# A Trainium2 attention-and-MLP kernel: another engine issues the folded-weight transfers, and some weight loads lose their fixed place in the order

## The chip, the cores and the metric

The kernel runs on one core of one Trainium2 chip. A core has five engines with instruction streams of their own: TensorE (PE in the rows; PEld is its weight load), VectorE (DVE), ScalarE (ACT), GpSimd (POOL) and SyncE (SP). Each runs its instructions in order and waits for the others on semaphores. Transfers run on 16 DMA engines; an instruction stream only issues them, and a wait that a transfer has before it can start is waited out by the engine that issues it. The metric is the device time of one execution in microseconds (us), lower is better.

## The reference

Per batch and head, 32 packed queries attend to 576 keys and values; the 576 queries then attend to the 32 results. The output, 4608 tokens of 512 features, goes through a gated MLP with RMS normalisation and then through a second MLP:

```python
p_packed = sm_attn(p, k, v)              # 8 batches, 8 heads, 32 x 576, head_dim 64
x = sm_attn(q, p_packed, p_packed)       # 576 x 32; then heads side by side: 4608 x 512
rms = np.sqrt(np.mean(x * x, axis=-1, keepdims=True) + 1e-06)
xn = x / rms * rms_g
g = xn @ w_gate                          # 512 x 1536
x = (g * (1.0 / (1.0 + np.exp(-g)))) * (xn @ w_val) @ w_out
h = x @ w_in                             # 512 x 2048
out = np.maximum(0.01 * h, h) @ w_out2   # 2048 x 512
```

## The kernel before

Every float32 product is made of three matmuls of a high and a low part (`mm3`: high by high, low by high, high by low). So each operand is split: ScalarE copies the high part (`act_copy`, line 129), VectorE or GpSimd subtracts it (line 137). Nearly all matmuls go through line 112 in `mm3`.

**Folded weights.** Attention ends in a product of the softmax weights of 576 queries with 32 packed values for each head. The kernel does not form that output: it multiplies the packed values (`lpw`) into the MLP's gate and value weights first (`pw_piece`) and gives the result, `pw`, to the matmuls `g` and `v` (`gv`), whose moving operand is the transposed softmax weights `ath`. The features come in 6 groups (fg) of 256 for each pair of batches, so n = 0 to 23 counts pair and group. For each n there are four pieces (i = 4n + kt). `pw_piece(i)` does three matmuls into the PSUM bank `pwps`, a ScalarE copy of the high part into the weight tile `w` that it just used, a VectorE subtract of the low part into the same tile, and two transfers, one for each half of the partitions (64 partitions x 4 KB, 256 KB), from `w` into `pw[n, 0]` and `pw[n, 1]`. Line 858 issues these: 96 pieces, 192 transfers. All four pieces of n must have landed before the first `g` matmul of n can run. Tile `w` has four buffers, so that a load of a later `w` (line 764) waits for the landing of the transfers out of an earlier one; `pw` has two buffers per batch of the pair, so the first writers of n + 2 wait for the last `v` of n.

**Stages.** The program has four stages. A (0 to about 530 us): the gated MLP for batches 0 to 3 (n = 0 to 11), in which the attention of these batches and the splitting of all weights of the first MLP and of half of the second (`split_w`, `split_wo`, `split_w2`, with loads on lines 742, 775, 764, 796, 813 and stores on line 655) are interleaved by slots. Z (530 to about 970 us): the second MLP for the first four chunks of 512 tokens, in two halves of its 2048 hidden features (`stage3z`: tiles `zh`, `zr`, `zgf`, `zgh`, `zgl`; `stage4z`: `zo`, `zob`, with partial sums stored to and loaded from `op_dram`), interleaved with the attention of batches 4 to 7 (tiles `s`, `e`, `ta`, `pp`, `xp`, `atf`). C (990 to about 1315 us): the gated MLP for batches 4 to 7 (n = 12 to 23), some 28 us for each n, in four steps of `g`, `v` and `y` (tiles `sg`, `hh`, `hl`, `y_acc`). D (1315 to 1776 us): the second MLP for the other five chunks (`h`, `o`).

**Second MLP's weights.** They are read back split from DRAM in parts of 1 MB (128 x 2048 float32): `load_part`, line 986, two parts for each of `w1[f]` and `w2[f]`, f = 0 to 3. The parts are put on a list, `trickle`, and `drop(1)` takes one at a time: in stage A and C at line 1233 (the fused loop over `g`, `v`, `y`), in Z behind each `stage3z` (the middle part), and in D behind each `stage4` (the last part). In the middle part w1[2], w2[2], w1[3] and w2[3] take the place of w1[0], w2[0], w1[1] and w2[1] in the same buffers. In the rows, w12 is w1[2], w22 is w2[2], and so on; a first digit or two of `zh`, `zo` and the like are the chunk-and-half s = 0 to 7 and then the feature tile m, so that zh410 is s = 4, m = 10.

**What sets the order.** The Python code gives a program order, and the Tile scheduler, which works with a model of the durations, orders each engine's instructions anew. An instruction given to `tc.keep_in_program_order` is pinned: it keeps its place in the program. `load_part` pins every load. SP issues all loads and stores, ScalarE only the 192 transfers of line 858.

Of the kernel before, what the change touches and what calls it, by code (L numbers as in the profile page):

```python
# [8 lines left out]
F32 = mybir.dt.float32  # L9
# [30 lines left out]
def pack_attention_moe_kernel(  # L40
# [14 lines left out]
    nc = tc.nc  # L55
# [50 lines left out]
    def mm3(ps, terms, start=True, stop=True):  # L106
        seq = [t for hi, lo in (("h", "h"), ("l", "h"), ("h", "l")) for t in [(hi, lo)]]
        n = len(terms) * 3
        i = 0
        for a, b in seq:  # L110
            for (lh, ll), (rh, rl) in terms:
                mm = nc.tensor.matmul(  # L112
                    ps,
                    lhsT=lh if a == "h" else ll,
                    rhs=rh if b == "h" else rl,
                    start=start and i == 0,
                    stop=stop and i == n - 1,
                )
                i += 1
        return mm  # L120
# [7 lines left out]
    def act_copy(o, i, scale=1.0):  # L128
        nc.scalar.activation(out=o, in_=i, func=AF.Copy, scale=scale)  # L129
# [6 lines left out]
    def sub(eng, o, a, hi):  # L136
        eng.tensor_tensor(out=o, in0=a, in1=hi.bitcast(F32), op=ALU.subtract)  # L137
# [67 lines left out]
    def bank(name):  # L205
        return psA.tile([P, 1, 512], F32, tag="y", bufs=ybufs, name=name)
# [445 lines left out]
    def flush_store():  # L652
        if stores:
            o, t = stores.pop()
            nc.sync.dma_start(out=o, in_=t.bitcast(F32))
# [67 lines left out]
    def until(done):  # L723
        while not done():
            assert drip
            drain(1)
# [103 lines left out]
    pw = {}  # L830

    def pw_piece(i):
        if i >= NPAIR * NFG * KT:
            return
        until(lambda: ("s", i) in wq)
        n, kt = i // KT, i % KT
        pr = n // NFG
        u, x = kt // 2, kt % 2
        if kt == 0:
            for bb in range(2):  # L840
                pw[n, bb] = mlpa.tile(
                    [P, 2, 2, 2 * G * P], F32R, tag=f"pw{bb}", bufs=2, name=f"pw{n}{bb}"
                )
        w = wq.pop(("s", i))
        wh, wl = w[:, 0, :], w[:, 1, :]
        lh, ll = lpw[pr]
        ps = bank(f"pwps{i}")[:, 0, :]
        mm3(ps, [((lh[:, kt, :], ll[:, kt, :]), (wh, wl))])

        if stores and stores[0][1] is w:  # L850
            flush_store()
        st = w
        act_copy(st[:, 0, :], ps)
        sub(nc.vector, st[:, 1, :], ps, st[:, 0, :])
        for half in range(2):
            bb = half if x == 0 else 1 - half
            hs = slice(64 * half, 64 * half + 64)
            nc.scalar.dma_start(out=pw[n, bb][hs, u].bitcast(F32), in_=st[hs].bitcast(F32))

    hid = {}  # L860

# [2 lines left out]
    def gv(n, bb, c, which, g, ps):  # L864
        w = pw[n, bb]
        ah, al = ath[2 * (n // NFG) + bb]
        cs = slice(c * CH, c * CH + CH)
        if g == 0:
            ps = psA.tile([P, G, 512], F32, tag=which, bufs=1, name=f"{which}{n}{bb}{c}")
        o = (0 if which == "g" else G * P) + g * P  # L870
        fs = slice(o, o + P)
        mm3(
            ps[:, g, :CH],
            [((w[:, u, 0, fs], w[:, u, 1, fs]), (ah[:, u, cs], al[:, u, cs])) for u in range(2)],
        )
        return ps
# [55 lines left out]
    for f_ in weights[:HOLD]:  # L932
# [6 lines left out]
        (split_wo, 0),  # L939
        (split_wo, 1),  # L940
        (pw_piece, 0),
        (pw_piece, 1),
        (split_w, 4),
        (pw_piece, 2),
        (split_w, 5),
        (pw_piece, 3),
# [30 lines left out]

    trickle = []

    def drop(count=1):  # L980
        for _ in range(min(count, len(trickle))):
            trickle.pop(0)()

    def load_part(t, src, k_):
        ks = slice(2 * k_, 2 * k_ + 2)
        ins = nc.sync.dma_start(out=t[:, ks].bitcast(F32), in_=src[:, ks])
        tc.keep_in_program_order(ins)

    def load_w1sb(pool, f, tag=None):
        tags = dict(tag=tag, bufs=1) if tag else {}  # L990
        t = w1[f] = pool.tile([P, 4, 2, 512], F32R, name=f"w1{f}", **tags)
        trickle.extend(lambda k_=k_: load_part(t, w1_dram[f], k_) for k_ in range(2))

    def load_w2sb(pool, f, tag=None):
        tags = dict(tag=tag, bufs=1) if tag else {}
        t = w2[f] = pool.tile([P, 4, 2, 512], F32R, name=f"w2{f}", **tags)
        trickle.extend(lambda k_=k_: load_part(t, w2_dram[f], k_) for k_ in range(2))
# [112 lines left out]
    for si, (n, bb, c) in enumerate(steps):  # L1110
# [20 lines left out]
        if si == 2 * 4 * NFG:  # L1131
# [25 lines left out]
            for z, (s_, m) in enumerate(za):  # L1157
# [7 lines left out]
                if z == 31:  # L1165
                    load_w1sb(zw2, 3, "w1")
                drop(1)
                if z == len(za) - 1:
                    zw2.release()
# [61 lines left out]
        if si == 3 * 4 * NFG + 16:  # L1231
            split_y(NZ)
        if si >= 2 * 4 * NFG or si % 2:
            drop(1)
        gps = gv(n, bb, c, "g", 0, None)
        more_y()
        gv(n, bb, c, "g", 1, gps)
# [93 lines left out]
    for n, (i, m) in enumerate(order):  # L1331
        stage3(i, m)
        if n >= 2:
            stage4(*order[n - 2])
        drop(1)
        if m == 2:
            load_y(i + 1)
        if m == 8:
            split_y(i + 1)
# [41 lines left out]
```

## Time and profile before

| | us |
|---|---|
| median of 3 runs | 1775.86 |
| lowest and highest | 1774.94, 1776.55 |
| profiled execution | 1777.73 |
| its span (first to last instruction) | 1775.9 |
| TensorE busy in it | 1676.8 (94%) |
| TensorE busy in stage A, 530 us | 462.97 |
| in stage Z, 460 us | 449.69 |
| in stage C, 325 us | 315.74 |
| in stage D, 461 us | 448.37 |

TensorE's busy time includes time at a lower granted clock, and what is not busy in it is idle time in front of a matmul. The profiled execution took 1777.73 us, of which 1.83 us lie outside the span, and it is 1.87 us above the median. Stages are windows of the trace at the times given above, which the profile does not name itself. Of a matmul that is issued late, the rows give the idle time of TensorE before it and the producer that ended it.

### The profile page before, as it was taken

To read this page: it belongs to the slowest core of one execution; us is meant where nothing else is said; L and a number is where in the kernel's file an instruction comes from. 1 tells how busy PE (TensorE), PEld (TensorE's weight loads), DVE (VectorE), ACT (ScalarE), POOL (GpSimd) and SP (SyncE) were. 2 spreads that over 40 slices of the span, in tenths; PEclk is the share of its full clock that TensorE was granted. 3 is DMA by queue.
4 is the path that set the end of the run, shared out by engine and by line. 5 is a ranking of instruction groups with operands and counts; after the bars stand their busy time and mean duration, and the time that the engine had idled before them with its cause. 6 is when DMAs were issued, how large, how long until landed. Compare 5 with 4: busy or idle time off the path is not lost.

```text
span 1775.9 us, 24117 instructions
## 1 busy us (share of the span) xinstructions
PE 1676.8 (94%) x9252; PEld 1475.1 (83%) x9252; DVE 911.2 (51%) x1560; ACT 648.7 (37%) x1144; POOL 373.0 (21%) x270
## 2 busy tenths in 40 slices
PE   6778899999899999989998999999999999999997
PEld 5568788989898888878887999989998888888885
DVE  7766788557548877666642244334443323232221
ACT  4344555443325555444332422242222222222221
POOL 2244354533322232212121211311110000000000
PEclk9799999999999999989999999999999999999998
DMA  9675777699948563453237656786635101010000
GB/s 293 204 224 147 226 215 226 204 336 300 362 122 280 166 202 126 150 211 105 69 108 239 193 165 202 218 262 181 175 136 238 32 17 34 15 33 15 12 12 24
DMA packets 95527, 287.85 MB, mean 162 GB/s; under 512 B 13876, under 2 KB 20276, under 8 KB 91316
## 3 DMA queue, kind: packets, MB, share of 16 engines
q1 hardware_dynamic: 80052, 235.96, 39.9%
q10 hardware_dynamic: 15360, 50.34, 11.4%
q8 instruction: 73, 1.20, 0.3%
q14 instruction: 42, 0.34, 0.1%
HBM read 174.85 MB, written 61.08 MB: 133 GB/s over the span
## 4 chain that ended last, share of the span: by engine, by line
PE 69%; DMA 18%; DVE 7%; issue 2%; ACT 2%; ACTq 1%; SPq 1%; POOL 0%; DVEq 0%; POOLq 0%
PE h L112 12%; PE o L112 12%; PE y L112 9%; PE zh L112 8%; PE zo L112 8%; PE g L112 6%; DMA pw<-w 6%; PE v L112 5%; PE pwps L112 2%; PE pp L335 2%; DMA out_dram<-zob 1%; PE s L112 1%; DMA w<-in_moe_w_val_dram 1%; DMA w<-in_moe_w_in_dram 1%; DMA y_dram<-y_acc 1%
## 5 line engine op out<-in xcount | busy, mean ns | idle before, releaser
L112 PE MATMUL y<-hh,wo 128*128 128x288 f32 x1536 | 271.2, 298 | 20.0 <-ACT y_acc L129 8.8
L112 PEld LDWEIGHTS y<-hh,wo 128*128 128x128 f32 x1536 | 226.6, 189 | 27.8 <-ACT y_acc L129 10.1
L137 POOL TENSOR_TENSOR hl<-sg,hh 128x576 fp32r<-128x576 f32 x96 | 140.2, 1460 | 406.6 <-ACT hh L129 397.2
L903 DVE TENSOR_TENSOR y_acc<-y_acc,y 128x288 f32<-128x288 f32 x320 | 141.6, 450 | 151.9 <-PE y L112 151.1
L112 PE MATMUL o<-w,gh 128*128 128x512 f32 x640 | 212.4, 392 | 0.0
L1293 DVE TENSOR_TENSOR gf<-r,h 128x512 f32<-128x512 f32 x80 | 55.0, 687 | 248.7 <-ACT r L129 248.7
L112 PE MATMUL zo<-w,zgh 128*128 128x512 f32 x512 | 172.3, 396 | 1.7 <-ACT zgh L129 1.7
L112 PE MATMUL g<-ath,pw 128*128 128x288 f32 x768 | 144.5, 304 | 25.7 <-DMA pw<-w 19.2
L112 PE MATMUL zh<-zyh,w 128*128 128x512 f32 x512 | 162.2, 394 | 3.1 <-DVE zgf L1049 1.9
L112 PE MATMUL h<-yh,w 128*128 128x512 f32 x640 | 162.5, 393 | 0.5 <-DVE y_acc L903 0.5
L112 PE MATMUL y<-hl,wo 128*128 128x288 f32 x768 | 161.7, 296 | 0.0
L112 PEld LDWEIGHTS g<-ath,pw 128*128 128x128 f32 x768 | 119.0, 193 | 35.4 <-issue 17.1
L112 PEld LDWEIGHTS h<-yh,w 128*128 128x128 f32 x640 | 120.0, 188 | 28.1 <-DVE y_acc L903 0.8
L129 ACT ACTIVATE r<-h 128x512 f32<-128x512 f32 x80 | 47.8, 598 | 261.1 <-PE h L112 261.1
L112 PEld LDWEIGHTS o<-w,gh 128*128 128x128 f32 x640 | 120.1, 188 | 27.2
L112 PE MATMUL v<-ath,pw 128*128 128x288 f32 x768 | 140.8, 300 | 0.6 <-ACT sq L538 0.3
L880 DVE TENSOR_TENSOR sg<-sg,v 128x576 f32<-128x576 f32 x96 | 72.1, 751 | 106.0 <-PE v L112 87.0
L112 PE MATMUL o<-w,gl 128*128 128x512 f32 x320 | 125.0, 391 | 0.0
L112 PEld LDWEIGHTS y<-hl,wo 128*128 128x128 f32 x768 | 123.0, 189 | 0.1
L129 ACT ACTIVATE hh<-sg 128x576 fp32r<-128x576 f32 x96 | 65.6, 683 | 150.5 <-DVE sg L880 133.7
L112 PEld LDWEIGHTS v<-ath,pw 128*128 128x128 f32 x768 | 116.5, 191 | 2.0 <-DVE sg L880 0.8
L1239 ACT ACTIVATE sg<-g 128x576 f32<-128x576 f32 x96 | 62.5, 651 | 148.8 <-PE g L112 110.4
(158 smaller groups left out, 3002.6 us busy)
## 6 DMA issues: line engine op xcount, KB each, us to landing
pw<-w ACTq DMA_DIRECT2D x192, 256.0 KB
w<-w_dram SPq DMA_DIRECT2D x72, 512.0 KB
w<-w_dram SPq DMA_DIRECT2D x32, 1024.0 KB
wo<-wo_dram SPq DMA_DIRECT2D x36, 512.0 KB
w_dram<-w2s SPq DMA_DIRECT2D x32, 512.0 KB
w_dram<-w SPq DMA_DIRECT2D x24, 512.0 KB
y_dram<-y_acc SPq DMA_DIRECT2D x32, 288.0 KB
w<-in_moe_w_in_dram SPq DMA_DIRECT2D x16, 512.0 KB
```

The costliest lines, as they stand in the source:

```text
L112: mm = nc.tensor.matmul(ps, lhsT=lh if a == "h" else ll, rhs=rh if b == "h" else rl, start=start and i == 0, stop=stop and i == n - 1,)
L129: nc.scalar.activation(out=o, in_=i, func=AF.Copy, scale=scale)
L137: eng.tensor_tensor(out=o, in0=a, in1=hi.bitcast(F32), op=ALU.subtract)
L335: nc.tensor.matmul(pp[:, 0, :256], lhsT=st["a1T"][:, j // 3, j % 3, :], rhs=vr[:, :, j, :], start=j == 0, stop=j == NJ - 1,)
L880: nc.vector.tensor_tensor(out=hf, in0=sg, in1=vps[:, :, :CH], op=ALU.mult)
L903: pace[:] = [nc.vector.tensor_tensor(out=ya, in0=ya, in1=pv, op=ALU.add).ins]
L1239: nc.scalar.activation(out=sg, in_=gps[:, :, :CH], func=AF.Silu)
L1293: pace[:] = [nc.vector.tensor_tensor(out=gf, in0=r, in1=ps, op=ALU.max).ins]
```

## The change

There are two edits. In `pw_piece` the two transfers of a piece are issued by SP (`nc.sync`) and no longer by ScalarE. And `load_part` no longer pins its load; `drop` pins it if it is told to, which only the fused loop does. So the loads that are dropped in the middle part (Z) and in the last part (D) are free for the scheduler to place, and those of the fused loop stay pinned.

```diff
-            nc.scalar.dma_start(out=pw[n, bb][hs, u].bitcast(F32), in_=st[hs].bitcast(F32))
+            nc.sync.dma_start(out=pw[n, bb][hs, u].bitcast(F32), in_=st[hs].bitcast(F32))
...
-    def drop(count=1):
+    def drop(count=1, pin=False):
         for _ in range(min(count, len(trickle))):
-            trickle.pop(0)()
+            ins = trickle.pop(0)()
+            if pin:
+                tc.keep_in_program_order(ins)
...
-        ins = nc.sync.dma_start(out=t[:, ks].bitcast(F32), in_=src[:, ks])
-        tc.keep_in_program_order(ins)
+        return nc.sync.dma_start(out=t[:, ks].bitcast(F32), in_=src[:, ks])
...
         if si >= 2 * 4 * NFG or si % 2:
-            drop(1)
+            drop(1, pin=True)
```

ScalarE's stream falls from 1296 to 1106 rows of the order, SP's rises from 515 to 711. The scheduler answers with another order on the other engines too: on TensorE some 2000 lines of the difference, small displacements of `g`, `v`, `y` and attention matmuls through stage A, larger ones from s = 4 on in Z, and in each n of C some of the first `g` of the next n moves ahead of some `y` matmuls. In stage D the order of every engine is what it was, the unpinned loads included. The line numbers of the changed kernel are higher by one or two behind the edit.

**SP in stage Z**, at the loads for the second half's weights (w12, w22, w13, w23; zob is the partial sum, at_dram<-atf5 the store of batch 5's normalised softmax weights, q, k, v the inputs of batches 6 and 7). Before:

```order
L1065 DMA zob41_7767<-op_dram_66 128x512
L1065 DMA zob42_7773<-op_dram_66 128x512
L1065 DMA zob43_7779<-op_dram_66 128x512
L986 DMA w23_7725<-w2_dram_64 128x2048
L594 DMA at_dram_65<-atf5_7387 128x1152
L162 DMA q61_7457<-in_q_dram 128x1152
L986 DMA w22_7459<-w2_dram_64 128x2048 x2
L164 DMA k71_7754<-in_k_dram 64x1152
L165 DMA k71_7754<-in_k_dram 64x1152
L184 DMA v70_7593<-in_v_dram 96x2x384
L185 DMA v70_7593<-in_v_dram 96x2x384
L986 DMA w13_7542<-w1_dram_63 128x2048 x2
```

Now, at the place where w12 and w22 stand:

```order
L1080 DMA op_dram_66<-zob22_6659 128x512
L1080 DMA op_dram_66<-zob23_6664 128x512
L988 DMA w12_7262<-w1_dram_63 128x2048 x2
L164 DMA p71_7757<-in_p_dram 64x64
L165 DMA p71_7757<-in_p_dram 64x64
L162 DMA q60_7075<-in_q_dram 128x1152
L988 DMA w22_7459<-w2_dram_64 128x2048
L164 DMA k70_7380<-in_k_dram 64x1152
L165 DMA k70_7380<-in_k_dram 64x1152
L988 DMA w22_7459<-w2_dram_64 128x2048
L182 DMA v61_7223<-in_v_dram 96x4x384
L1023 DMA zyl43_7549<-y_dram_60 128x512
```

The load w22 stood behind the store of atf5 and the load q61, and it now stands in front of v61, some twenty rows of SP earlier; w13 and w23 moved up in the same way, and w12 went from behind v61 to right behind the last op_dram store of s = 2.

**TensorE at the same place**, where the zo matmuls of s = 4 start to read w22 (s2, ta61 and pp61 are attention of batch 6). Before:

```order
L112 MATMUL s260_1_7462<-qh60_7453,Ph60_7237 128x288 x2
L112 MATMUL s260_1_7462<-qh60_7453,Pl60_7238 128x288 x2
L112 MATMUL s260_1_7462<-ql60_7454,Ph60_7237 128x288 x2
L323 MATMUL ta61_0_7558<-ident_88,e161_7411 96x128 x3
L323 MATMUL ta61_1_7559<-ident_88,e161_7411 96x128 x3
L335 MATMUL pp61_7584<-v61_7223,a1T61_7557 128x256 x6
L112 MATMUL zo40_7760<-w22_7459,zgh48_7622 128x512
L112 MATMUL zo40_7760<-w22_7459,zgl48_7623 128x512
L112 MATMUL zo40_7760<-w22_7459,zgh48_7622 128x512
L112 MATMUL zo41_7766<-w22_7459,zgh48_7622 128x512
L112 MATMUL zo41_7766<-w22_7459,zgl48_7623 128x512
```

Now:

```order
L112 MATMUL zh413_7931<-zyh43_7602,w13_7542 128x512 x2
L112 MATMUL zh413_7931<-zyl43_7549,w13_7542 128x512
L112 MATMUL zo40_7760<-w22_7459,zgh411_7823 128x512
L112 MATMUL zo40_7760<-w22_7459,zgl411_7824 128x512
L335 MATMUL pp61_7584<-v61_7223,a1T61_7557 128x256 x6
L112 MATMUL zo40_7760<-w22_7459,zgh411_7823 128x512
L112 MATMUL zo41_7766<-w22_7459,zgh411_7823 128x512
L112 MATMUL zo41_7766<-w22_7459,zgl411_7824 128x512
L112 MATMUL zo41_7766<-w22_7459,zgh411_7823 128x512
L112 MATMUL xp060_0_7646<-ATh60_7580,Pmh60_7576 128x288
L112 MATMUL xp060_0_7646<-ATh60_7580,Pml60_7577 128x288
```

Before, the scores s260, the transpose ta61 and the product pp61 stood in one block between zh411 and the first zo; now zo and zh matmuls stand between them, and pp61 comes among the zo matmuls of m = 11.

**SP between Z and C**, at the loads for the first folded weights of n = 12 (w48 to w51) and the softmax weights of batch 4 (atr4). Before:

```order
L764 DMA w48_8823<-w_dram_61 128x1024
L764 DMA w49_8825<-w_dram_61 128x1024
L764 DMA w50_8884<-w_dram_61 128x1024
L764 DMA w51_8930<-w_dram_61 128x1024
L1008 DMA out_0_dram<-zob60_8737 4x32x512
L632 DMA atr4_8818<-at_dram_65 128x1152
L1008 DMA out_0_dram<-zob61_8743 4x32x512
L1008 DMA out_0_dram<-zob62_8749 4x32x512
L1008 DMA out_0_dram<-zob63_8755 4x32x512
L1065 DMA zob70_9125<-op_dram_66 128x512
L1065 DMA zob71_9131<-op_dram_66 128x512
L1065 DMA zob72_9137<-op_dram_66 128x512
```

Now:

```order
L1066 DMA zob72_9137<-op_dram_66 128x512
L1066 DMA zob73_9143<-op_dram_66 128x512
L594 DMA at_dram_65<-atf7_8777 128x1152
L764 DMA w48_8823<-w_dram_61 128x1024
L764 DMA w49_8825<-w_dram_61 128x1024
L764 DMA w50_8884<-w_dram_61 128x1024
L764 DMA w51_8930<-w_dram_61 128x1024
L632 DMA atr4_8818<-at_dram_65 128x1152
L858 DMA pw120_8874<-w48_8823 64x1024
L858 DMA pw121_8875<-w48_8823 64x1024
L858 DMA pw121_8875<-w49_8825 64x1024
L858 DMA pw120_8874<-w49_8825 64x1024
```

The store of atf7 and the loads w48 to w51 and atr4 now stand behind the four output stores zob60 to zob63 and the four loads zob70 to zob73 (the first two rows are the last of these), and the transfers of pieces 48 and 49 stand behind atr4.

**SP in stage C**, n = 13 to 14 (w56 to w63 are plain loads, pw140 and pw141 the two tiles of n = 14). Before:

```order
L764 DMA w56_9547<-w_dram_61 128x1024
L764 DMA w57_9557<-w_dram_61 128x1024
L764 DMA w58_9699<-w_dram_61 128x1024
L764 DMA w59_9776<-w_dram_61 128x1024
L796 DMA wo28_9701<-wo_dram_62 128x1024
L796 DMA wo29_9778<-wo_dram_62 128x1024
L764 DMA w60_9853<-w_dram_61 128x1024
```

Now:

```order
L764 DMA w56_9547<-w_dram_61 128x1024
L764 DMA w57_9557<-w_dram_61 128x1024
L858 DMA pw130_9399<-w54_9409 64x1024
L858 DMA pw131_9400<-w54_9409 64x1024
L858 DMA pw131_9400<-w55_9470 64x1024
L858 DMA pw130_9399<-w55_9470 64x1024
L764 DMA w58_9699<-w_dram_61 128x1024
L764 DMA w59_9776<-w_dram_61 128x1024
L858 DMA pw140_9689<-w56_9547 64x1024
L858 DMA pw141_9690<-w56_9547 64x1024
L764 DMA w60_9853<-w_dram_61 128x1024
```

The loads of w keep their order, and the transfers of the pieces now stand among them, each behind the loads that the row before it names.

## Rows read from the trace of the kernel before

**Rows 1.** Windows by stage: us, busy PE PEld DVE ACT POOL, PE clock, DMA share, GB/s.

```profile
0.00:530.00 530.00, 462.97 (x2886) 422.46 (x2887) 363.42 (x658) 232.77 (x412) 200.89 (x151) 0.96 0.77 238
530.00:990.00 460.00, 449.69 (x2151) 378.43 (x2150) 286.39 (x468) 207.03 (x380) 102.19 (x70) 0.99 0.52 167
990.00:1315.00 325.00, 315.74 (x2256) 308.30 (x2255) 130.91 (x241) 95.03 (x164) 68.48 (x48) 0.99 0.64 188
```

**Rows 2.** The waits view of TensorE in stage A: time in all, times, longest.

```profile
PE g L112 <- DMA pw<-w: 12.6, 8, 2.5
PE y L112 <- ACT y_acc L129: 8.8, 5, 4.5
...
PE g L112 <- ACT sg L1239: 4.8, 5, 1.4
```

**Rows 3.** The windows view of three short stretches of Z.

```profile
757.00:774.00 17.00, 11.86 (x40) 8.84 (x39) 13.39 (x23) 5.15 (x9) 3.70 (x3) 0.70 0.92 331
...
940.00:957.00 17.00, 13.04 (x48) 9.77 (x47) 5.17 (x8) 6.13 (x11) 3.24 (x2) 0.90 0.93 228
957.00:974.00 17.00, 15.79 (x80) 13.23 (x79) 5.44 (x9) 3.77 (x6) 0.00 (x0) 1.00 0.81 297
```

**Rows 4.** TensorE's timeline: start, us, line, operation, count, idle before and releaser.

```profile
15.29 2.86 PE L335 MATMUL pp<-v,a1T 96*128 96x256 f32 x12 [0.90 <-ACT a1T L129]
...
120.80 0.79 PE L112 MATMUL y<-hh,wo 128*128 128x288 f32 x4 [4.51 <-ACT y_acc L129]
...
765.10 1.53 PE L323 MATMUL ta<-ident,e 128*96 128x128 f32 x6 [2.76 <-ACT e L308]
766.57 5.49 PE L335 MATMUL pp<-v,a1T 96*128 96x256 f32 x12
...
942.69 0.73 PE L112 MATMUL zh<-zyh,w 128*128 128x512 f32 x2 [1.87 <-DVE zgf L1049]
```

**Rows 5.** The timeline of SP at seven places; SPq is its queue of issues.

```profile
263.87 0.39 SPq L655 DMA_DIRECT2D wo_dram<-wo  x1
...
760.90 0.32 SPq L594 DMA_DIRECT2D at_dram<-atf  x1
...
762.52 0.94 SPq L986 DMA_DIRECT2D w<-w_dram  x2
...
918.98 2.33 SPq L764 DMA_DIRECT2D w<-w_dram  x4
...
930.91 12.50 SPq L1065 DMA_DIRECT2D zob<-op_dram  x4
...
1134.81 3.97 SPq L906 DMA_DIRECT2D y_dram<-y_acc  x3
...
1167.17 1.32 SPq L986 DMA_DIRECT2D w<-w_dram  x2
```

**Rows 6.** The timeline of ScalarE at six places; ACTq is its queue of issues.

```profile
114.70 5.08 ACTq L858 DMA_DIRECT2D pw<-w  x3
...
259.20 2.90 ACTq L858 DMA_DIRECT2D pw<-w  x4
...
941.32 0.60 ACT L129 ACTIVATE zr<-zh 128x512 f32<-128x512 f32 x1 [6.45 <-DMA out_dram<-zob]
...
943.27 4.23 ACTq L858 DMA_DIRECT2D pw<-w  x4
...
1132.36 2.93 ACTq L858 DMA_DIRECT2D pw<-w  x4
...
1166.11 3.29 ACTq L858 DMA_DIRECT2D pw<-w  x4
```

**Rows 7.** The waits view of TensorE in stage C.

```profile
PE g L112 <- DMA pw<-w: 6.6, 8, 2.3
```

**Rows 8.** The page, third part: queues, packets, MB, share of 16 engines.

```profile
q1 hardware_dynamic: 80052, 235.96, 39.9%
q10 hardware_dynamic: 15360, 50.34, 11.4%
```

## The prediction

> **What bounds the kernel now.** The windows by stage come first [rows 1]. TensorE is busy 462.97 of 530 us in A, 449.69 of 460 in Z and 315.74 of 325 in C, so the idle time that any edit can win is 67 us in A, 10.3 in Z and 9.3 in C; D keeps its order on every engine, so I give it nothing. Beside idle time there is time at a lower granted clock, which counts as busy: 0.96 in A, 0.99 elsewhere. The waits of TensorE then tell which of this idle time the moved instructions touch. In A, 12.6 us in 8 waits end with a transfer into pw, and 13.6 us end with a ScalarE output (y_acc 8.8, sg 4.8) [rows 2]; in C, 6.6 us in 8 waits end with a transfer into pw [rows 7]. The short windows of Z show where its 10.3 us lie [rows 3]: 5.1 between 757 and 774, where the clock was 0.70, 4.0 between 940 and 957, at 0.90, and 1.2 in the next 17 us. The rest of A's 67 us waits for the attention's own chain and for splitting steps, which keep their work.
>
> **The unpinned loads, stage Z.** SP issued the load of w22 at 762.52, behind the store of atf5 at 760.90 [rows 5]; the first zo of s = 4 reads w22 and cannot start before, and TensorE had only the attention of batch 6 in front of it. It waited 2.76 us for ta61's operand alone and ran pp at 5.49 us for 12 matmuls, where the same 12 took 2.86 early in the trace [rows 4]. In the window, 17.00 - 11.86 = 5.1 us are idle, and of the 11.86 busy some 0.30 x 11.86 = 3.6 are lost to the clock, which fell behind the idle gaps: 8.7 us [rows 3]. In the new order w22 is issued some 40 us sooner, right behind the k loads, and zo and zh matmuls stand between s260, ta61 and pp61. The waits for softmax steps then lie under zo and zh matmuls that have all they need. I take -9. Ends: -4, if the interleaved attention matmuls still wait as long as the one gap of 2.76 and keep part of the clock down, and -10.2 (5.1 idle and 0.30 of all 17 us). Nothing is late next: TensorE is busy without a gap on either side of this window, and the store of atf6 is needed only in C.
>
> **Unpinned loads, last part.** The order of D is the same with and without pins: 0, one answer.
>
> **The end of Z.** Here both edits meet. Before, ScalarE stood behind its own pw issues: they waited until 940.80, and zr came 6.45 us late; then four issues held it 4.23 us more from 943.27 [rows 6]. TensorE stood 1.87 us at 942.69 [rows 4] and 4.0 idle in the window, with a clock of 0.90 that cost 0.10 x 13 = 1.3: with the 1.2 us idle in the next 17, some 6.5 us can go [rows 3]. What is put in its place: w48 to w51 and atr4 stand behind the stores zob60 to zob63 and the loads zob70 to zob73, which SP took 12.5 us to issue from 930.91 on [rows 5], each load waiting for a store to land. In the new order piece 48 has only some 53 matmuls (about 10.5 us at 15.79 us / 80 [rows 3]) between it and the first g of n = 12, and ScalarE's stream has the copies of atr4 and atr5 ahead of zgh. Were the four loads zob70 to zob73 issued up to 943.4 as before, w48 would come out behind them where it was at 918.98 [rows 5]. From such rows I estimate 2 to 5 us of waiting for w48 and 1.5 to 3 for the copies, together 6.5 against the 6.5: 0. Ends: -5 (the new waits are hidden but for 1.5) and +6 (both new waits near their upper ends, 8, and only 2 of the old ones gone).
>
> **The queue, stage C.** ScalarE has little to do there (95.03 of 325 us [rows 1]), so its freed time is worth nothing. What counts is when the last transfer of an n is issued. Four issues took 2.90 us on ScalarE, at 259.20 [rows 6]; four plain loads took 2.33 us on SP [rows 5], which is 0.5 to 0.6 less. In the eight waits for pw [rows 7] that wins at most 0.5 each, and some are shorter than that: about -3. Against it: SP is not always free. The pieces 74 and 75 stand behind a y_dram store that SP issued at 1134.81, where ScalarE issued them at 1132.36: +2 of that, since the n that follows waits for them. The pieces 78 and 79 stand behind two 1 MB loads for D that SP issued from 1167.17 to 1168.49, where ScalarE issued them from 1166.11 on: 2.4 later, but those loads shared the DMA engines with them already; I take +1 [rows 5, 6]. Sum: -3 + 3 = 0. Ends: -6.6 (all of the waits) and +6 (both cases in full, 2.45 + 2.4, and 1 us at one more n).
>
> **The queue, stage A.** ScalarE's issues waited for the subtract or for a free buffer and held up everything behind them: three at 114.70 took 5.08 us [rows 6], and TensorE stood 4.51 us at 120.80 for y_acc [rows 4], which ScalarE writes behind them. Four of the five y_acc waits follow such issues, so of the 13.6 us I take -6, about half, since the copies behind them have other waits too. The waits for pw win 0.5 each, 8 times: -4. Against it, SP's queue is busy with loads that wait: the pieces that ScalarE issued at 259.20 stand behind a wo_dram store of 263.87 [rows 5, 6], 4.7 us later, in front of an n that waited for pw already: +5. Sum: -5. Ends: -18 (13.6 and 4 of the pw waits) and +10 (two more such places); the reshuffled attention is inside these.
>
> **A rule that speaks against the queue.** The rows show two queues in use, one of 235.96 MB from SP and one of 50.34 MB from ScalarE [rows 8], at 238 GB/s in A [rows 1]. On one queue a piece issued behind two 512 KB loads would start only after them, about 1 MB / 238 GB/s = 4.4 us, an estimate for a queue strictly in order; but such loads then no longer compete with it, so I put it at nothing and keep it in A's end of +10. The Trainium skill, "DMA: Bandwidth & Descriptors", section "Issuing engines are not separate DMA queues", says that issuing from several engines at once saves only the issue time on the sequencer; by that rule nothing of the transfers changes and only the issue time is regained, which would leave the time to Z alone: rival 1 below. The trace agrees as far as it goes: four issues cost 2.90 us on ScalarE [rows 6]; what the transfers do on one queue no row of before shows.
>
> **Sum.** -9 + 0 + 0 - 5 = -14 us on the profiled execution of 1777.73 us, or 1763.7; that execution lies 1.87 above the median, so 1762 as a median, 0.8% below 1775.86.
>
> **The rivals.** (1) Z alone: the queue change is neutral, its gains in A met by SP's hold-ups, and only the 757 window goes: -9, about 1767. For it speaks the rest of A's idle time, which has the attention's chain behind it; against it the 4.51 us gap that sits right behind ScalarE's issues. (2) No change: the end of Z comes out at +6, C at +2 and A at 0, which leaves -1 of the 9: about 1775. For it: w48 is issued behind eight transfers that wait for one another. Against it: before, the same stretch already lost 6.5 us to ScalarE's queue, which goes in any case. (3) Slower: SP holds the pieces back. SP stands in order, and its loads and stores wait for landings; where such a wait stands ahead of a fourth piece, all of TensorE's next n waits. One such place costs 2.45 to 4.7 us (the two pairs of rows above), and there are 24 n. The sum above holds 5 us of it in A and 3 in C. Each further n held by 3.5 us takes a quarter of the forecast's 14: with four more the time is that of before, and with eight more it is -14 + 28 = +14, or 1790. It decides from the fifth on. For it: many of SP's loads and stores in A wait for splitting steps, as that of 263.87 does. Against it: in C most loads of w that wait stand behind the very pieces whose landing they wait for, and so hold nothing up.
>
> **How the numbers follow.** Forecast (-10 to -25 us) 0.45, rival 1 (-4 to -10) 0.24, rival 2 0.12, rival 3 0.19. A measurement of this kernel can tell 0.2%, or 3.6 us, from no change. So faster 0.69, same 0.12, slower 0.19. Range: from 1749 (-27: the 757 window at -10, A halfway to its better end at -11, the end of Z and C at -3 each) up to 1780, which takes in rival 2 and the smaller half of rival 3.
>
> **What would show it.** Right: no gap of TensorE above 1 us and a clock of 1.00 where zo of s = 4 starts; the y_acc and sg waits of A fall from 13.6 to about 7; ScalarE never idle behind an issue. The waits for pw show the rest: 12.6 in A and 6.6 in C should stay about equal. Wrong: if they grow by more than 10 us, rival 3 holds; if TensorE stands more than 7 us between Z and C, the end of Z was mis-sized; if A's busy share moves by 10 us for attention waits, the reshuffle and not the queue decides.

## The result

The changed kernel is slower. Ten executions gave a median of 1785.49 us (1779.18 to 1798.55), ten of the kernel before 1775.4 (1765.81 to 1789.13); the ratio is 1.0054 with a 95% interval of 1.0029 to 1.0079, so some 10 us (0.5%) lost where I forecast 14 won. The profiled execution of the changed kernel took 1798.55 us (span 1796.8), the longest of its ten: its gaps are larger than those of a median execution, and their place is what is read from them.

The page of the changed kernel, first, third and fourth part:

```profile
PE 1684.1 (94%) x9252; PEld 1485.2 (83%) x9252; DVE 910.4 (51%) x1560; ACT 652.1 (36%) x1144; POOL 376.2 (21%) x270
...
q1 hardware_dynamic: 95412, 286.31, 51.1%
...
PE h L112 12%; PE o L112 12%; PE y L112 10%; DMA pw<-w 8%; PE zo L112 7%; PE zh L112 7%; PE g L112 7%; PE v L112 6%; PE pwps L112 2%; DMA wo<-in_moe_w_out_dram 2%; DMA w<-in_moe_w_in_dram 1%; PE s L112 1%; PE pp L335 1%; SPq L858 1%; DVE cvw L685 1%
```

One queue now carries all of the 286.31 MB that two carried [rows 8], and on the chain that ended last the transfers into pw take 8% of the span. The waits view of TensorE over the whole span, then over stage C and stage A; the last line is stage A before:

```profile
PE g L112 <- DMA pw<-w: 50.7, 16, 6.5
...
PE g L112 <- DMA pw<-w: 30.3, 10, 6.5
...
PE g L112 <- DMA pw<-w: 14.2, 5, 5.4
PE y L112 <- DVE w L137: 6.5, 8, 1.9
PE y L112 <- ACT y_acc L129: 3.1, 3, 1.6
...
PE y L112 <- DVE w L137: 2.4, 5, 0.7
```

In A the y_acc waits fell from 8.8 to 3.1 and those behind sg are no longer in the list, while the waits for pw are 14.2 against 12.6 [rows 2], as forecast; a wait that I had not counted, of y for VectorE's subtract of a w, grew from 2.4 to 6.5. In C the waits for pw, 6.6 before [rows 7], are 30.3, and one more of 6.2 us stands ahead of the window, at n = 13. The windows that answer to those of before, the one between 757 and 774 first, then stage C up to about 1343, then two short ones behind gaps of TensorE:

```profile
757.00:774.00 17.00, 17.00 (x84) 14.47 (x83) 14.16 (x22) 7.51 (x13) 3.36 (x2) 1.00 0.43 140
...
953.00:1343.00 390.00, 352.97 (x2437) 344.45 (x2438) 140.12 (x256) 105.67 (x181) 73.96 (x52) 0.95 0.61 176
...
1052.00:1055.00 3.00, 3.00 (x14) 3.00 (x14) 0.45 (x1) 0.65 (x1) 0.00 (x0) 0.50 0.14 52
...
1115.51:1119.00 3.49, 3.49 (x26) 3.49 (x27) 0.51 (x2) 0.65 (x1) 0.00 (x0) 1.00 0.59 193
```

The stretch that had 5.1 us of idle time at a clock of 0.70 [rows 3] is full at 1.00. In C some 37 of 390 us are idle, and the clock stands at 0.95 where it was 0.99 [rows 1]. Ten waits for pw from n = 13 on are longer than 1 us, and behind seven of them the granted clock falls for some microseconds to 0.50, the lower of its two levels: so behind the gap of 4.33 us that ended at 1049.66, but not behind that of 2.89 us that ended at 1115.51.

The loss can be placed further. Each g, zh and h matmul of the trace belongs to a known n, s and m, since TensorE keeps its program's order; the time between such matmuls splits the span into stretches that can be compared between kernels. These are the profiled executions of all the kernels below, in us (n = 12 begins C, h begins D):

| kernel | issues pieces of A / C | Z loads | n = 2 to zh of s = 0 | s = 3 to s = 7 | s = 7 to n = 12 | n = 12 to 15 | n = 15 to h | h to end |
|---|---|---|---|---|---|---|---|---|
| before | ScalarE / ScalarE | pinned | 365.4 | 228.6 | 59.6 | 82.7 | 268.6 | 454.4 |
| e1 | ScalarE / ScalarE | free | 367.2 | 216.3 | 60.5 | 86.5 | 265.4 | 454.0 |
| e10 (e1 again) | ScalarE / ScalarE | free | 366.5 | 216.7 | 61.3 | 86.6 | 271.1 | 454.0 |
| e8 | SP / ScalarE | pinned | 359.6 | 228.8 | 62.2 | 82.8 | 265.0 | 454.0 |
| e3 | SP / ScalarE | free | 365.7 | 216.3 | 59.0 | 88.5 | 265.8 | 454.0 |
| e2 | SP / SP | pinned | 365.9 | 227.6 | 58.2 | 88.0 | 292.9 | 454.0 |
| changed | SP / SP | free | 362.9 | 216.3 | 57.8 | 90.6 | 299.2 | 454.0 |
| e4 | SP / SP, w loads held | free | 358.1 | 216.5 | 57.7 | 92.1 | 270.8 | 454.0 |
| e5 | SP / SP, one w load held | free | 358.9 | 216.5 | 57.5 | 90.4 | 266.0 | 454.0 |
| e11 (e5 again) | SP / SP, one w load held | free | 359.7 | 216.7 | 57.8 | 89.7 | 264.0 | 454.0 |
| e6 | SP / SP at n = 12, then ScalarE | free | 359.2 | 216.7 | 57.5 | 89.7 | 267.9 | 454.0 |
| e7 | as e4, ScalarE at n = 13 | free | 357.5 | 216.3 | 57.0 | 93.7 | 271.5 | 454.0 |

Two stretches are left out: up to n = 2 (164.1 us before, 161.7 in the changed kernel, 157.3 to 166.3 in all of them), and from s = 0 to s = 3, which takes 152.5 or 152.6 us with pinned loads and 153.2 to 155.4 with free ones. And the order moves some matmuls across the borders. With free loads 16 attention matmuls (`xp`, `ms`) of 0.13 us, 2.1 us in all, come behind the first zh of s = 7 and no longer ahead of it. With SP from n = 0 on, 13 matmuls come ahead of n = 2 and no longer behind it (some 2 us, an estimate from 0.23 us for each of three pwps and 0.13 for the others). With SP in C, six y matmuls of 0.13 us come behind the first g of n = 15.

Read across the changed kernel: up to s = 0, where both kernels have run the same matmuls, it is 4.9 us ahead (524.6 and 529.5). It loses 1.7 us from s = 0 to s = 3, wins 12.3 between s = 3 and s = 7 (10.2 for the same matmuls), 1.8 at the end of Z (3.9 for the same matmuls) and 0.4 in D; 7.9 are lost in n = 12 to 14, and 30.6 in the rest of C, 3.4 us for each n in the mean, from 0.4 at n = 20 to 6.9 at n = 15. So both edits won what they were forecast to win, about, and the queue lost more in C. The windows of the kernel before and of the changed one from n = 15 on tell what the loss is made of:

```profile
1053.00:1321.00 268.00, 260.83 (x1861) 254.62 (x1859) 111.00 (x206) 75.71 (x129) 58.46 (x41) 0.99 0.62 185
...
1043.00:1343.00 300.00, 271.79 (x1873) 265.63 (x1872) 112.83 (x209) 76.63 (x129) 58.30 (x41) 0.95 0.59 170
```

Of the 32 us between these windows some 21 are idle time of TensorE (7.2 and 28.2) and some 11 busy time, at 0.95 of the clock in place of 0.99.

One n shows how. The timeline of SP in the changed kernel, from the second piece of n = 17 to the fourth (68 to 71; the two pw rows are pieces 69, then 70 and 71, the load at 1106.63 is w73). Behind it the same pieces before, on ScalarE, and SP's four loads w72 to w75:

```profile
1096.53 0.33 SPq L764 DMA_DIRECT2D w<-w_dram  x1
1096.91 0.90 SPq L796 DMA_DIRECT2D wo<-wo_dram  x2
1098.31 1.11 SPq L858 DMA_DIRECT2D pw<-w  x2
1106.63 0.33 SPq L764 DMA_DIRECT2D w<-w_dram  x1
1107.00 3.10 SPq L858 DMA_DIRECT2D pw<-w  x4
...
1096.70 1.12 ACTq L858 DMA_DIRECT2D pw<-w  x2
...
1103.75 2.87 ACTq L858 DMA_DIRECT2D pw<-w  x4
...
1094.60 17.10 SPq L764 DMA_DIRECT2D w<-w_dram  x4
```

ScalarE's copies of pieces 70 and 71, VectorE's subtracts for them, and the g matmuls of n = 17, of which all but the first wait, in the changed kernel's timeline; the last row is the g that waits before:

```profile
1104.02 1.29 ACT L129 ACTIVATE w<-pwps 128x512 fp32r<-128x512 f32 x2
...
1104.65 1.39 DVE L137 TENSOR_TENSOR w<-pwps,w 128x512 fp32r<-128x512 f32 x2 [0.87 <-ACT w L129]
...
1110.88 0.29 PE L112 MATMUL g<-ath,pw 128*128 128x288 f32 x1
...
1115.51 0.63 PE L112 MATMUL g<-ath,pw 128*128 128x288 f32 x3 [2.89 <-DMA pw<-w]
...
1111.43 0.63 PE L112 MATMUL g<-ath,pw 128*128 128x288 f32 x3 [0.16 <-DMA pw<-w]
```

The section on the kernel says that the first g of an n needs all four pieces. It does not: it reads the first two, and the next g the last two. So the first g of n = 17 ran at 1110.88, and the wait came behind it.

Tile w73 takes the buffer of w69, so its load waits until piece 69 has landed, 8.3 us after that was issued. In the program it stands behind piece 71 (`pw_piece(j)`, then `split_w(j + 2)`); the scheduler drew it ahead of piece 70 on SP. Piece 70's tile was ready at about 1105.3 (half of the subtracts), and its transfer was issued at 1107.00. Over C, these loads are what SP waits for most. The last line is C before: SP waited even longer for the same loads, but no piece stood behind them.

```profile
SPq L764 <- DMA pw<-w: 133.2, 39, 9.8
SPq L858 <- DVE w L137: 76.7, 18, 9.5
...
SPq L764 <- DMA pw<-w: 152.1, 39, 11.2
```

### The profile page after: what moved, and what is told of

It reads as the page before. It is cut to its first block, busy times and chain, and to the rows that moved or that the text cites. A ratio compares the mean times of both kernels' runs of the same rounds, so it can differ in the third digit from the quotient of the medians.

```text
span 1796.8 us, 24145 instructions
## 1 busy us (share of the span) xinstructions
PE 1684.1 (94%) x9252; PEld 1485.2 (83%) x9252; DVE 910.4 (51%) x1560; ACT 652.1 (36%) x1144; POOL 376.2 (21%) x270
## 3 DMA queue, kind: packets, MB, share of 16 engines
q1 hardware_dynamic: 95412, 286.31, 51.1%
## 4 chain that ended last, share of the span: by engine, by line
PE 69%; DMA 17%; DVE 8%; issue 2%; ACT 2%; SPq 1%; POOL 1%; DVEq 0%; ACTq 0%; POOLq 0%
PE h L112 12%; PE o L112 12%; PE y L112 10%; DMA pw<-w 8%; PE zo L112 7%; PE zh L112 7%; PE g L112 7%; PE v L112 6%; PE pwps L112 2%; DMA wo<-in_moe_w_out_dram 2%; DMA w<-in_moe_w_in_dram 1%; PE s L112 1%; PE pp L335 1%; SPq L858 1%; DVE cvw L685 1%
## 5 line engine op out<-in xcount | busy, mean ns | idle before, releaser
L112 PE MATMUL g<-ath,pw 128*128 128x288 f32 x768 | 149.5, 312 | 52.7 <-DMA pw<-w 50.7
L112 PEld LDWEIGHTS g<-ath,pw 128*128 128x128 f32 x768 | 123.3, 199 | 61.9 <-issue 38.2
L112 PEld LDWEIGHTS h<-yh,w 128*128 128x128 f32 x640 | 120.0, 188 | 28.2 <-DVE y_acc L903 0.8
L112 PEld LDWEIGHTS v<-ath,pw 128*128 128x128 f32 x768 | 120.4, 198 | 2.2 <-DVE sg L880 1.6
```

Of the source, the lines that this page charges most:

```text
L112: mm = nc.tensor.matmul(ps, lhsT=lh if a == "h" else ll, rhs=rh if b == "h" else rl, start=start and i == 0, stop=stop and i == n - 1,)
```

## The experiments

**One edit alone, e1 and e2.** e1_unpin_only is the changed kernel with

```diff
-            nc.sync.dma_start(out=pw[n, bb][hs, u].bitcast(F32), in_=st[hs].bitcast(F32))
+            nc.scalar.dma_start(out=pw[n, bb][hs, u].bitcast(F32), in_=st[hs].bitcast(F32))
```

> Only the second edit: loads of the middle and last part unpinned, ScalarE goes on issuing the pieces. Theory (the unpinned loads win the gap where zo of s = 4 starts, and the lost time of the changed kernel lies in stage C and comes from SP's queue): the gap of 757 to 774 goes, some 9 us faster than before, about 1766, and the waits of g for pw in C stay at 6 to 8 us. Rival (the new order of TensorE, not the queue, makes C slow): C takes some 20 to 30 us more here too, and the time is 1780 or above.

e2_queue_only is the kernel before with the opposite line.

> Only the first edit: SP issues the pieces, all loads stay pinned. Theory: stage C is as slow as in the changed kernel (waits of g for pw there 30 us or more), the gap at 757 to 774 stays, A wins about 5: about 1790 to 1797, slower than the changed kernel by what the unpinned loads win. Rival (the new order makes C slow): about 1770, C as before.

e1 took 1775.49 us against 1778.26 of the kernel before on the same chip, a ratio of 0.9982 (0.9959 to 1.0006); e2 took 1794.21, 1.0091 (1.0063 to 1.012). (Each ratio is an estimate of its own, and differs by up to 0.23% from the quotient of the two medians.) The loss goes with the queue's edit: the waits for pw in C, of e1 and then of e2, are

```profile
PE g L112 <- DMA pw<-w: 5.4, 5, 1.6
...
PE g L112 <- DMA pw<-w: 32.0, 9, 7.7
```

e1 has the new place of the loads in Z, and TensorE's new order there, and C is as before; e2 has neither, and C is as slow as in the changed kernel. These two leave one rival: from n = 15 on, TensorE's order in e1 is that of the kernel before, and in e2 that of the changed kernel, so queue and order move together here. e5 below separates them. Against expectation, e1's time fell by 3 us and not by 9, with an interval that takes in no change. Since its profiled execution was the shortest of its twelve (6.8 of its 13.5 us lie ahead of n = 2), it was run again.

> The kernel of e1_unpin_only once more. In the profiles so far every kernel with unpinned loads takes 216.3 to 216.7 us from the first zh of s = 3 to the first of s = 7, m = 8, and every kernel with pinned loads 227.6 to 228.8, so 12 us; but the times of e1_unpin_only gave only 3 us with an interval from 7 faster to 1 slower. Theory (the 12 us are kept): the ratio is near 0.994, some 10 us faster. Rival (they are given back at the end of Z or in C, where ScalarE still issues the pieces): a ratio of 0.998 again, with more waits there than in the first profile.

The second result was the same: 1775.28 against 1777.07, 0.9983 (0.9962 to 1.0004). The rival holds in the main: the 12 us are won in Z in both profiles (216.3 and 216.7 against 228.6), and 2.1 of them are the 16 matmuls that come later. Of the 10 that are left, 2.6 and 0.9 are given back between s = 0 and s = 3 and 3.8 and 3.9 in n = 12 to 14; the end of Z, 0.9 and 1.7 longer, holds the 16 matmuls and gives nothing back. That leaves some 4 to 5, inside the intervals of both ratios. The timelines of TensorE and of ScalarE in e10 show waits at the end of Z and in n = 13:

```profile
955.28 2.07 PE L112 MATMUL zo<-w,zgh 128*128 128x512 f32 x4 [3.56 <-ACT zgh L129]
...
987.90 0.93 PE L112 MATMUL y<-hh,wo 128*128 128x288 f32 x4 [3.14 <-ACT y_acc L129]
...
982.95 4.43 ACTq L858 DMA_DIRECT2D pw<-w  x4
987.43 0.71 ACT L129 ACTIVATE y_acc<-y 128x288 f32<-128x288 f32 x2 [6.79 <-DMA pw<-w]
```

TensorE comes to the end of Z and to n = 13 sooner than the transfers do, and ScalarE, which issues them, stands in front of its own zgh and y_acc meanwhile.

**SP in A, ScalarE in C, e3, and with the loads pinned, e8.** Both choose the queue by n:

```diff
+            eng = nc.sync if n < 2 * NFG else nc.scalar
-            nc.sync.dma_start(out=pw[n, bb][hs, u].bitcast(F32), in_=st[hs].bitcast(F32))
+            eng.dma_start(out=pw[n, bb][hs, u].bitcast(F32), in_=st[hs].bitcast(F32))
```

> The changed kernel, but ScalarE issues the pieces of n = 12 to 23, SP those of n = 0 to 11. Theory: it keeps what the changed kernel has won by n = 12 (17 us in the profiled execution) in part, and C is as before, with 6 to 8 us of waits for pw: 1758 to 1764, faster than both. Rival (end of Z is won only because SP issues pieces 48 to 51): about 1768, with the end of Z as before. Rival (order makes C slow): 1780.

> The kernel before (all loads pinned) with SP issuing the pieces of n = 0 to 11 only. Theory (SP in A wins some 5 to 12 us, and the unpinned loads the 3 to 7 that lie between this kernel and e3_queue_a_only): 1766 to 1773. Rival (A's gain is an accident of e3_queue_a_only, or belongs to the unpinned loads): 1776 to 1780, as before.

e3: 1762.88, 0.9913 (0.9882 to 0.9944). e8: 1771.72 against 1779.98, 0.9968 (0.9945 to 0.9991). So SP in A wins some 6 us by itself, and undoing the queue in C turns the changed kernel's 1.0054 into 0.9913: C's pieces on SP cost 25 us, and 22 with the loads pinned (e2 and e8). In the table the stretch of A takes 365.4 to 367.2 in the three profiles with ScalarE and 357.5 to 365.9, 360.8 in the mean, in the nine with SP (e6 and e7 below among them); some 2 us of this difference are the 13 matmuls that moved. From the start to s = 0 the three take 524.5 to 530 us, 528.0 in the mean, and the nine 519 to 532, 523.7 in the mean: 4 us, with a spread that is larger. Whether the queue wins them or TensorE's order in A, which moves with it in all nine, no run separates.

**What on SP costs it, e4 and e5.** In the changed kernel, loads of w from n = 14 on are held behind the last piece issued so far in the program; e4_hold_w holds the first two of each n:

```diff
+    last_pw = []
...
-            nc.sync.dma_start(out=t.bitcast(F32), in_=w_dram[i % NW])
+            held = last_pw and i >= 2 * NW + 8 and i % 4 < 2
+            with tc.issue_after(last_pw[0]) if held else nullcontext():
+                nc.sync.dma_start(out=t.bitcast(F32), in_=w_dram[i % NW])
...
-            nc.sync.dma_start(out=pw[n, bb][hs, u].bitcast(F32), in_=st[hs].bitcast(F32))
+            last_pw[:] = [nc.sync.dma_start(out=pw[n, bb][hs, u].bitcast(F32), in_=st[hs].bitcast(F32)).ins]
```

> The changed kernel, SP issues all pieces, but from n = 14 on the loads of the first two w tiles of an n are issued behind the transfers of the piece that stands two pieces ahead of them in the program, so that no such load waits for a landing in front of the third and fourth piece, nor in front of the wo loads. Theory (SP stands behind a load that waits for the landing of the second piece, 2.5 us or more per n, and the wo loads are bunched in front of the second piece): the waits of g for pw in C fall from some 30 us to under 10 and the time to 1758 to 1765. Rival (one queue: the pieces lie behind loads in the DMA engines and land later whatever the order of the waits): the waits stay at 20 us or more, and the time above 1775.

e5_hold_w1 differs in `i % 4 == 1`: only the load that stood ahead of the third piece (w73 above) moves behind the fourth.

> As e4_hold_w, but only the second of the w loads (the one that waits for the landing of the second piece and stood in front of the third and fourth) is held back; the first one still waits for the landing of the first piece in front of the two wo loads. Theory (SP's wait in front of the third and fourth piece is the larger part of what C lost): about 1768 to 1772, some three quarters of what e4_hold_w won over the changed kernel, waits for pw in C 1.5 to 2.5 us per n. Rival (the bunched wo loads in front of the second piece are the larger part): above 1778.

e4: 1766.07, 0.9924 (0.9894 to 0.9954). e5: 1760.03, 0.9911 (0.9886 to 0.9936), no worse than e4 (the intervals overlap), where I expected three quarters of its gain. e4's waits for pw, 12.7 us, did not fall under the 10 that I expected. Moving this one load of each n cures all of the loss from n = 15 on (264.0 and 266.0 us against 268.6 before and 299.2), with the same engine issuing the same transfers on the same queue. TensorE's order is not the cause either: from n = 15 on, the first g of an n and the next one have 11 matmuls between them in e5 as in the changed kernel (n = 19 apart, 13 and 40), where the kernel before mostly has 7. In e5 they start 1.58 us apart where nothing waits; in the changed kernel it is 4.63 at n = 17, 2.89 of it the wait. e5 was run again, beside e10.

> The kernel of e5_hold_w1 once more, beside it, for the better version: theory, that SP can issue all the pieces at no cost in C once no load that waits for a landing stands in front of the third and fourth piece: a ratio of 0.989 to 0.993 again, 5 us or more below e10_unpin_again. Rival: the first result was a good draw, and it is equal to e10_unpin_again.

e11: 1758.3 against 1777.07, 0.9875 (0.9843 to 0.9906); e10 beside it 0.9983. The version that holds one load is faster than both kernels: by its two ratios 16 to 22 us below the kernel before. SP's timeline in e11 at the same pieces of n = 17, and the waits for pw in its stage C:

```profile
1077.54 1.11 SPq L862 DMA_DIRECT2D pw<-w  x2
1082.71 0.33 SPq L768 DMA_DIRECT2D w<-w_dram  x1
1083.08 0.91 SPq L800 DMA_DIRECT2D wo<-wo_dram  x2
1084.56 9.95 SPq L862 DMA_DIRECT2D pw<-w  x6
1094.62 0.55 SPq L768 DMA_DIRECT2D w<-w_dram  x1
...
PE g L112 <- DMA pw<-w: 6.5, 4, 2.2
```

The four transfers of pieces 70 and 71 follow those of 69 with no load between, and w73 is issued at 1094.62, behind them. What this load costs where it stood has two parts: SP's wait in front of piece 70 and the issue of the load, some 1.7 us here (1105.3 to 1107.00), and its 512 KB ahead of the piece in the queue. e4 bears on the second part: there another load, w72's kind, has its buffer free and stands between the third and the fourth piece. SP's rows of w72 and of piece 71 in e4, and its waits for pw in C, are

```profile
1097.25 0.57 SPq L768 DMA_DIRECT2D w<-w_dram  x1
1097.86 1.67 SPq L862 DMA_DIRECT2D pw<-w  x2
...
PE g L112 <- DMA pw<-w: 12.7, 9, 2.5
```

0.9 to 1.3 us in six of the eight n from 15 to 22, where e5 waits in two and e11 in three. So a 512 KB load ahead of the last piece costs something without any wait of SP's. But 0.6 us of it is the issue of the load (1097.25 to 1097.86), and e4's order has 19 matmuls between the first g and the next, where e5 has 11, so these waits do not give the price of the bytes. How the 21 us of idle time of the changed kernel divide between SP's wait and the bytes isn't settled. For n = 17 alone, the g that waits came 5.4 us behind the end of the last issue (1110.10 to 1115.51), where it came 4.8 us behind it before (1106.62 to 1111.43), so SP's 1.7 us are the larger part there. A load with a free buffer in the place of w73's would tell more, and was not tried.

**The end of Z and n = 13, e6 and e7.** e6_queue_to_12 lets ScalarE issue from n = 13 on (`n <= 2 * NFG` in e3's line), e7_hold_w_13 is e4 with ScalarE issuing n = 13 alone.

> The changed kernel with SP issuing the pieces of n = 0 to 12 and ScalarE those of n = 13 to 23. Theory: C from n = 13 on as in the kernel before, and the ScalarE stalls at the end of Z of e3_queue_a_only (zgh 3.0, sg 0.6, y_acc 2.0, pw 1.7) go too: 3 to 7 us below e3_queue_a_only, about 1757. Rival (the end of Z is even between the two queues, as I forecast): equal to e3_queue_a_only, about 1763.

> As e4_hold_w, with ScalarE issuing the four pieces of n = 13 alone, which on SP stand behind the output stores of the last chunk of Z. Theory (these stores held the first g of n = 13 by 6.4 us): 5 to 7 us below e4_hold_w, about 1760. Rival (TensorE waits there for something else that is as late): equal to e4_hold_w, about 1766.

e6: 1761.78, 0.9906 (0.9876 to 0.9936), equal to e3. e7: 1767.03, 0.995 (0.9924 to 0.9976), no better than e4: both rivals hold. In the changed kernel, e4 and e5 alike the first g of n = 13 waits over 6 us for piece 53; in e7 that wait is gone and TensorE stands at other places, as the first two rows of its timeline show; the third is TensorE's wait in the changed kernel:

```profile
979.10 0.80 PE L112 MATMUL y<-hh,wo 128*128 128x288 f32 x4 [3.50 <-ACT y_acc L129]
...
1016.70 0.67 PE L112 MATMUL g<-ath,pw 128*128 128x288 f32 x3 [3.11 <-DMA pw<-w]
...
979.73 0.58 PE L112 MATMUL g<-ath,pw 128*128 128x288 f32 x1 [6.17 <-DMA pw<-w]
```

n = 12 to 14 take 86.5 to 93.7 us in the profile wherever the loads of Z are free or SP issues the pieces there, and 82.7 and 82.8 where neither is so. What these n wait for in common I haven't settled; that the DMA engines have a backlog there (eight loads, the output stores and the pieces in some 20 us) is only argued.

## Why the prediction was wrong

- **The unpinned loads, stage Z: right.** -9 forecast; -11.9 to -12.3 between s = 3 and s = 7 in every profile with free loads, 2.1 of it matmuls that moved, so -9.8 to -10.2, at the better end that I gave; the window has no gap and a clock of 1.00. What I missed is that part of it is given back, in s = 0 to 3 and at n = 12 to 14: alone the edit is worth 3 us and not 9 (0.9982 and 0.9983). Beside SP's queue it is worth 7 us (e2 and the changed kernel) and 10 (e8 and e3), which the intervals do not tell from 3.
- **The last part: right.** D takes 454.0 us in all, 454.4 before.
- **The queue, stage A: the sum right, its terms not.** -5 forecast; 0.9968 in e8, -5.7 us (-1.6 to -9.8). But the y_acc and sg waits fell by 10.5 us where I took 6, and y's wait for VectorE's subtract, which I had left out, grew by 4.1, so part of the agreement is luck. The end of +10 does not follow from its terms: two more places of 4.7 us take -5 to +4.4.
- **The end of Z: missed in both halves, and they cancel in part.** Up to n = 12 it is 3.9 us shorter for the same matmuls, against 0 forecast and an end of -5. The new waits come, but later: n = 12 to 14 take 7.9 us more, 8.7 with the six y matmuls that moved out, together +4.8, near the end that I gave (+6).
- **The queue, stage C: this step failed.** Forecast 0 with ends at -6.6 and +6; measured +30.6 in the profile from n = 15 on, and 25 us between e3 and the changed kernel by the ratios. I had priced two places where SP holds a piece back, n = 18 at +2 and n = 19 at +1; the waits there grew by 3.9 and 4.2 us, and five other n were held as well. Two sentences behind the step were wrong. First, that SP issues the four transfers in 0.5 us less than ScalarE: its row shows 3.10 us (2.86 in e5, at 1118.03) where ScalarE took 2.90 and 2.93 [rows 6]. I had taken the price of plain loads of another form [rows 5]. Second, and larger, the sentence against the third rival: that "most loads of w that wait stand behind the very pieces whose landing they wait for, and so hold nothing up". SP's rows above show w73 behind the transfers out of w69, whose landing it waits for, with the transfers out of w70 and w71 next, which were ready (1105.3 and 1106.0) before w69's had landed (1106.63); so it is with one such load in each n from 14 to 22. In n = 23, which loses only 0.8 us, no load stands there. I looked at what the load stands behind and not at what stands behind the load. The third piece's copy follows the second's by 7.1 us (1096.96 and 1104.02 on ScalarE), and the landing takes 8.3, with 1.5 MB of loads issued just ahead of it.
- **The rivals.** The third, SP holds the pieces back, is what happened, at 2.3 to 6.9 us for each n held, around the 3.5 that I gave. I gave it 0.19, with eight held n beyond those in the sum for a time of 1790; it acts in seven of the nine n from 15 on. The rule that I weighed, a piece behind loads on one queue, is not settled: e4 shows some 1 us behind a 512 KB load, 0.6 of it the issue. By the Trainium skill, "DMA: Bandwidth & Descriptors", section "Issuing engines are not separate DMA queues", only issue time is saved by issuing from a second engine. The trace agrees for the transfers themselves: e5 and e11, all on SP, take 266.0 and 264.0 us from n = 15 on, and the kernel before, with two engines, 268.6. What the second engine saved in the kernel before was a wait: SP's waits for landings, 152.1 us in C, did not hold ScalarE's transfers.

## What to carry to other kernels

When transfers move to another engine's stream, write down for every waiting instruction there what it waits for, when that comes, and which of the moved transfers stand behind it; a load that waits for the landing of one transfer and stands ahead of the next one can turn an even stream into a chain of landings. The place that counts is the one the scheduler gives it, not the one in the program. If one such load is all that is in the way, move that load behind the last transfer that is urgent and leave the rest. A gap that is closed early in a program counts only as far as the stage behind it can start earlier too.

## What was not expected of the hardware

The price of an issue went with the form of the transfer here, not with the engine: the two issues of a piece took 1.11 us on SP and 1.12 on ScalarE in their undisturbed form, where a plain 512 KB load took SP 0.33. And two 256 KB transfers from SBUF to SBUF landed 5.2 us after their issue in e11 (piece 68, 1077.54 to the load at 1082.71 that waits for it) and 8.3 us in the changed kernel (piece 69, 1098.31 to 1106.63) with 1.5 MB of loads issued in the 1.8 us ahead of them.
